# mLSTM cell and gelu layer on one core: DRAM copies moved from the up to the end of the down projection, and a new order of the down's steps

## The chip, the core and the metric

The kernel runs on one core of a Trainium2 chip. A core has a matrix engine (TensorE, in the profile PE, with PEld for its weight loads), a vector engine (VectorE, DVE), an activation engine (ScalarE, ACT), a general engine (GpSimd, POOL) and SyncE (SP), which here issues every DMA. Each engine runs its own instructions strictly in the order in which the program lists them, and waits on semaphores for the others. SP is such a queue too: a DMA that has to wait keeps back every DMA listed behind it.

The metric is the device time of one execution in microseconds (us). The kernel before took 484.46 us, the median of 3 runs (484.13 to 487.07).

## The reference

An mLSTM cell for 4 batches, 8 heads, 768 time steps and a head dimension of 40, and behind it a layer that widens 320 to 2048, applies the exact gelu and comes back to 320:

```python
for t in range(S):
    m_new = np.maximum(f_gate[:, :, t] + m, i_gate[:, :, t])
    f_stab = np.exp(f_gate[:, :, t] + m - m_new)
    i_stab = np.exp(i_gate[:, :, t] - m_new)
    C = f_stab[..., None, None] * C + i_stab[..., None, None] * einsum('bhd,bhe->bhde', vt, kt)
    n = f_stab[..., None] * n + i_stab[..., None] * kt
    y[:, :, t] = sigmoid(o_gate[:, :, t]) * (C @ qt) / maximum(abs(n . qt), 1.0)
x = y.transpose(0, 2, 1, 3).reshape(3072, 320)
out = gelu_exact(x @ w_in) @ w_out
```

## The kernel before

**Chunks.** Time is cut into 6 chunks of 128 steps. For each chunk the cell is computed in matrix form for each of the 4 batches: scores of keys and queries, times a weight matrix with a mask; times the values; plus what the carried state gives. Its output (512 rows of x) then goes through the layer: the up projection (`up`, L818: TensorE at L839 and L850, gelu on ScalarE at L854) and the down projection (`down_steps`, L907: TensorE at L920). While the down of chunk c runs, the cell of chunk c+1 is worked in between its products. For c = 1 to 4 the order of that mixture is written out by hand in the string DOWN (L37); the last down has no cell beside it. The profile shows the five pairs one after another: up and down of chunk 1 from 129.4 to 200.3 us, of chunk 2 to 274.5, of chunk 3 to 350.0, of chunk 4 to 419.5, and of chunk 5 to the end. What stands before 129.4 (the order FRONT) is the same before and after.

**The letters of DOWN.** Each word is a step, with a batch number behind it where it has one:

- F: the next of 14 products of the down (16 groups of rows summed in a Strassen-like scheme, 8 matmuls by 2 tiles). Every second F ends a bank of PSUM, and what empties it follows: F2 a copy on ScalarE (`p1`), F4 an addition on VectorE (`p6`), F6 a copy (`p2`), F8, F10, F12, F14 additions (`p5`, `p7`, `p3`, `p4`). `p3` and `p4` also issue two output DMAs each on SP (`send`, L887).
- M: the mask (GpSimd, L421). W: the exponentials of the weights (ScalarE, L447). G: the sigmoid of the output gate (ScalarE, L453).
- K and Q: VectorE transposes a batch's keys or queries (L469) from the tile `blocks`, one buffer for the batches 0, 1 and 2. Q of the batches 0 and 1 also issues the loads of the next batch's blocks (4 DMAs, L170); Q0 to Q2 and D3 weigh the values (GpSimd, L504). L3 clears a tile for the last batch (GpSimd, L459) and loads its blocks (4 DMAs). B3 loads the last batch's weights (L187). K and Q of the batches 0 and 1 do not stand in DOWN: they run in the up before it (`turns`), K0 and Q0 in its middle, K1 and Q1 later.
- S (scores of two batches: L533 on TensorE, then 8 multiplications on VectorE, L539), C (the old state times the queries, L588), h (the state's update: L599 on TensorE, L608 and L614 on VectorE, L612 on GpSimd). V: the values (TensorE L635, one addition on VectorE L643). V0 also issues the loads of the last batch's keys and values (4 DMAs, L152), into the buffers that batch 0 had.
- Y: the division (ScalarE L650, GpSimd L651 and L652, VectorE L656 and L657, then a copy on ScalarE, L664). X: the transposes of the result (TensorE L675, then a copy on ScalarE, L685). R: two operations of VectorE that split it in two parts (L698, L699). Z: two instructions of a sum of weights (VectorE, L753), in the down of chunk 1 alone. N: two subtractions on VectorE (`sum_late`, L950) that F11 and F12 need.
- j (`load_next`, L481): the loads of the first batch's blocks of the chunk after, 4 DMAs.

**The copies.** The blocks are read from a copy of k and q in DRAM with a fitting layout. `copy_chunk(c)` (L157) makes it for one chunk with 16 DMAs on SP (L162), 80 KB each. Chunk 2 is copied around the first up. In the up of chunk c the copy for chunk c+2 is issued (L864), for c = 1, 2 and 3: behind K0 and Q0 and behind the loads that the last down put off (`later_loads`: weights L190, keys and values L152 and L154, output gates L154), and ahead of the blocks that Q1 and L3 load.

Of the kernel before, what the change touches and what calls it, by code (L numbers as in the profile page):

```python
# [34 lines left out]
    K K B8 F J K F F J K F F F R0 X1 J J K F J F K X2 F J  # L35
    K F J Y3 K F R1 e J F Z B9 B10 F X3 R2 Z R3 F p"""
DOWN = """  # L37
    Z F M1 M0 W0 W1 F L3 Z Z S0 C0 F h0 B3 K2 G1 V0 Q2 M2 W2 G2 F K3 F M3 G0 V1 F W3 Q3 S2 D3 Y0 C2 h2 F Z G3 N F
    Y1 X0 F V2 F V3 X1 Y2 R0 F Y3 R1 j F X2 R2 F X3 R3 F"""


@with_exitstack
def kernel(
# [20 lines left out]
    NCH = S // L  # L64
# [92 lines left out]
    def copy_chunk(c, batches=range(B)):  # L157

        for b in batches:
            for i, src in enumerate((k, q)):  # L160
                for hip in range(2):
                    nc.sync.dma_start(out=kq_d[c - 2][b, hip].rearrange("(m i x t) d -> i x m (t d)", m=NP, i=2, x=16)[i],  # L162
                                      in_=src[b, hip::2, c * L:(c + 1) * L, :].rearrange("m (x t) d -> x m (t d)", x=16))

    def load_blocks(n, to):

        c, b = divmod(n, B)
        for hip in range(2):
            for d, w in ((0, 32), (32, D - 32)):
                nc.sync.dma_start(out=to[64 * hip + d:64 * hip + d + 32].rearrange("t m i (g w) -> t (m i g) w", w=32)[:, :, 0:w],  # L170
                                  in_=kq_d[c - 2][b, hip, :, d:d + w].rearrange("(x t) d -> t x d", t=32))
# [235 lines left out]
    class Cell:  # L407
# [73 lines left out]
        def load_next(self):  # L481
            if self.c + 1 < NCH:
                load_blocks((self.c + 1) * B, by_block)

        def weigh_last(self, b):
            if self.c < NCH - 1:
                self.weigh_values(b)
# [235 lines left out]
    def split_weight():  # L723
        i = len(w_lo)
        if i in (0, 3, 5, 8):
            two = shared([P, NX, 2, WP // 2], F32R, "w_in_hi")
            w_hi.extend([two[:, 0], two[:, 1]])
        elif i == 2:
            two = shared([P, 2, 2, WP // 2], F32R, "w_rest_hi")
            w_hi.append(two[:, 0])  # L730
            rest_two.append(two[:, 1])
        elif i == 7:
            w_hi.append(rest_two[0])
        w = w_all[i]
        nc.scalar.activation(out=w_hi[i], in_=w, func=AF.Copy, scale=PART * 2.0 ** -12)
        w_lo.append(w_f(F32R, "w_in_lo"))
        nc.vector.scalar_tensor_tensor(out=w_lo[i], in0=w_hi[i], scalar=-BASE * 2.0 ** 12, in1=w, op0=OP.mult, op1=OP.add)
# [3 lines left out]
    def join_weight(i):  # L741
        w_mid[i] = raw.tile([P, 2, WP // 2], F32R, name="w_in_mid", tag="pow") if i % 5 in (1, 4) else w_f(F32R, "w_mid")
        nc.vector.tensor_tensor(out=w_mid[i], in0=w_hi[i], in1=w_lo[i], op=OP.add)  # L743
# [22 lines left out]
    def hidden_sums(g, f0, f1):  # L766

        (a11, a21), (_, a22) = [[g.t[:, HF * e + f0:HF * e + f1, HT * h:HT * (h + 1)] for h in range(2)]
                                for e in range(2)]
        s1, s2 = [t[f0 // (HF // 2)][:, f0 % (HF // 2):f0 % (HF // 2) + f1 - f0, :] for t in (g.s1, g.s2)]  # L770
        nc.vector.tensor_tensor(out=s1, in0=a21, in1=a22, op=OP.add)  # L771
        nc.vector.tensor_tensor(out=s2, in0=s1, in1=a11, op=OP.subtract)
        nc.vector.tensor_tensor(out=a21, in0=a11, in1=a21, op=OP.subtract)
# [44 lines left out]
    def up(g, sums_too, turns):  # L818

        def split_to(i):  # L820
            while len(w_lo) <= i:
                split_weight()

        def pair(f, ahead):

            at = [f // 2 * 5 + f % 2 * 3 + x for x in range(NX)]
            split_to(at[1])
            for i in at:
                if i not in w_mid:
                    join_weight(i)  # L830
            pus = [[pool.tile([P, TG], F32, name="pu", tag=tag) for e in range(2)]
                   for pool, tag in (((ps_h, "h"), (ps_mm, "a")), ((ps_tr, "tr"), (ps_mm, "b")))[f % 2]]
            ahead()
            mid = [w_mid.pop(i) for i in at]
            for n, (w, x) in enumerate((([w_hi[i] for i in at], parts["x"]), ([w_lo[i] for i in at], parts["x_lo"]), (mid, parts["x_all"]))):
                for i in range(2):
                    for e in range(2):
                        for k in range(NX):
                            nc.tensor.matmul(pus[i][e], w[k][:, e, i * P:(i + 1) * P], x[:, k, :],  # L839
                                             start=(n == 0 and k == 0), stop=False, skip_group_check=True)  # L840
            return pus

        def rest(u, banks, order):
            mid = w_mid.pop(5 * u + 2)
            for i in order:
                pu = banks[i]
                for n, (w, x) in enumerate(((w_hi[5 * u + 2], parts["x"]), (w_lo[5 * u + 2], parts["x_lo"]), (mid, parts["x_all"]))):
                    for e in range(2):
                        r = halves[e]
                        nc.tensor.matmul(pu[e], w[r, i // 2, i % 2 * P:(i % 2 + 1) * P], x[r, NX, :], start=False,  # L850
                                         stop=(n == 2), skip_group_check=True)

        def out(i, e, pu):
            nc.scalar.activation(out=g.t[:, HF * e + i, :], in_=pu[e], func=AF.Gelu, scale=4097.0)  # L854

        if c == 1:
            copy_chunk(2, range(1, B))
        b0 = pair(0, lambda: split_to(4))
        b1 = pair(1, lambda: join_weight(2))
        for step in turns[:1]:  # L860
            step()
        while later_loads:
            later_loads.pop(0)()
        if c + 2 < NCH:  # L864
            copy_chunk(c + 2)
        rest(0, b0 + b1, (0, 1, 2, 3))
        split_to(6)
        join_weight(5)
        join_weight(6)
        for i, pu in enumerate(b0 + b1):  # L870
            for e in range(2):
                out(i, e, pu)
        for step in sums_too[:5]:
            step()
        b2 = pair(2, lambda: split_to(9))
        hidden_sums(g, 0, 2)
        b3 = pair(3, lambda: (hidden_sums(g, 2, 4), join_weight(7)))
        for step in turns[1:] + sums_too[5:]:
            step()
        rest(1, b2 + b3, (2, 3, 0, 1))  # L880
        for i, e in ((2, 0), (2, 1), (3, 0), (0, 0), (1, 0), (3, 1), (0, 1), (1, 1)):
            out(4 + i, e, (b2 + b3)[i])
        hidden_sums(g, HF - 2, HF)
        hidden_sums(g, HF - 4, HF - 2)
# [125 lines left out]
    for c in range(1, NCH):  # L1010
        g, later, steps = Hidden(True), [], {}
        if c + 1 < NCH:
            steps = cell_steps(c + 1, "MWGTscVYXRLKQDCBSjh", g)
        up(g, weight_sum(1) + weight_sum(2) + weight_sum(3) if c == 1 else [], [lambda b=b: (steps["K"](b), steps["Q"](b)) for b in range(2)] if steps else [])
        if c == 1:
            later = weight_sum(4)
        products, late = down_steps(c, g)
        steps |= dict(F=in_turn(products), Z=in_turn(later), N=late)
        play("F " * 14 if c + 1 == NCH else DOWN, steps)
# [30 lines left out]
```

## Time and profile before

| | |
|---|---|
| median of 3 runs | 484.46 us |
| the profiled execution's own time | 483.82 us |
| its span, first to last instruction | 482.0 us |
| mean granted TensorE clock | 0.996 |
| TensorE busy | 469.9 us (97%) |
| VectorE busy | 316.1 us (66%) |
| ScalarE busy | 244.1 us (51%) |
| GpSimd busy | 78.8 us (16%) |
| an up (chunk 2, 3, 4) | 28.72 us each |

The profile is of one execution. Its own time is 1.8 us above its span, which is what lies around the first and last instruction. "Idle, released by" tells who ended a wait. The chain of waits follows the run back from its last instruction; "SPq" in it is SP issuing DMAs. PE busy does not mean that TensorE is at its peak, only that a matmul was under way.

### The profile page before, as it was taken

What the parts mean: (1) busy time and instruction counts of PE and PEld (TensorE: products, weight loads), DVE (VectorE), ACT (ScalarE), POOL (GpSimd) and SP (SyncE); (2) the same over time, 40 slices, a digit from 0 to 9 for tenths busy, and PEclk for the clock granted to TensorE, in tenths of its full rate; (3) what the DMA queues carried; (4) which work ended last, traced back from release to release, by engine and by line L of the source; (5) the groups of instructions that cost most, each with busy time, mean ns of one, the idle gap of its engine ahead of it and who ended that gap; (6) DMA issues with size and microseconds to landing.
All of it is one profiled execution on the core that took longest, in us unless ns stands there. A gap on an engine that the chain in (4) does not pass through costs nothing.

```text
span 482.0 us, 12967 instructions
## 1 busy us (share of the span) xinstructions
PE 469.9 (97%) x5380; PEld 406.7 (84%) x5380; DVE 316.1 (66%) x694; ACT 244.1 (51%) x521; POOL 78.8 (16%) x120
## 2 busy tenths in 40 slices
PE   8899999999999999999989999989999999999997
PEld 8787888777777999977979977979977899977997
DVE  7899699797869958644747735647545767624321
ACT  6977999844532973231962211954303784211300
POOL 3002020000030223102324202215101412100000
PEclk9999999999999999999999999998999999999999
DMA  9997972278854640169590139582029930100001
GB/s 176 201 222 171 237 177 69 84 194 182 187 113 117 99 59 3 55 103 201 119 136 6 56 72 202 126 135 30 29 49 214 116 74 3 47 12 0 1 1 54
DMA packets 172475, 49.79 MB, mean 103 GB/s; under 512 B 154400, under 2 KB 165952, under 8 KB 172416
## 3 DMA queue, kind: packets, MB, share of 16 engines
q1 hardware_dynamic: 172416, 48.97, 50.7%
q8 instruction: 42, 0.69, 0.6%
q14 instruction: 17, 0.14, 0.1%
HBM read 44.82 MB, written 9.37 MB: 112 GB/s over the span
## 4 chain that ended last, share of the span: by engine, by line
PE 84%; SPq 6%; DVE 4%; DMA 2%; issue 2%; ACT 1%; POOL 0%; DVEq 0%
PE po L920 29%; PE pu L839 21%; PE po L897 7%; PE pu L784 6%; PE pu L850 5%; PE ph L635 3%; PE ps L533 2%; SPq L162 2%; PE px L675 2%; PE pu L790 2%; DMA blocks<-kq_d 2%; PE ps L517 2%; SPq L170 1%; PE pf L588 1%; SPq L154 1%
## 5 line engine op out<-in xcount | busy, mean ns | idle before, releaser
L854 ACT ACTIVATE g<-pu 128x512 f32<-128x512 f32 x80 | 40.8, 616 | 107.7 <-PE pu L850 107.6
L920 PE MATMUL po<-w_out,g 128*128 128x160 f32 x640 | 92.7, 301 | 0.0
L920 PEld LDWEIGHTS po<-w_out,g 128*128 128x128 f32 x640 | 87.9, 190 | 2.3 <-ACT g L854 1.8
L920 PE MATMUL po<-w_sums,sums 128*128 128x160 f32 x320 | 47.0, 303 | 0.0
L920 PEld LDWEIGHTS po<-w_sums,sums 128*128 128x128 f32 x320 | 43.9, 190 | 0.6
L839 PE MATMUL pu<-x_hi,w_in_hi 128*128 128x512 f32 x160 | 41.4, 401 | 0.0
L839 PE MATMUL pu<-x_lo,w_in_lo 128*128 128x512 f32 x160 | 40.6, 396 | 0.0
L447 ACT ACTIVATE W<-W,aT 128x128 f32<-128x128 f32 x128 | 38.7, 388 | 0.4
L839 PEld LDWEIGHTS pu<-x_hi,w_in_hi 128*128 128x128 f32 x160 | 29.4, 188 | 8.2 <-ACT g L854 1.9
L839 PEld LDWEIGHTS pu<-x_lo,w_in_lo 128*128 128x128 f32 x160 | 30.1, 188 | 7.2
L421 POOL TENSOR_SCALAR_AFFINE_SELECT W<-W 128x1024 f32<-128x1024 f32 (+2 forms) x20 | 22.2, 1111 | 80.6 <-DMA W<-M_d 72.6
L897 PE MATMUL po<-w_out,g 128*128 128x320 f32 x128 | 35.2, 433 | 0.0
L743 DVE TENSOR_TENSOR w_in_mid<-w_in_hi,w_in_lo 128x512 fp32r<-128x512 f32 x20 | 13.8, 688 | 29.5 <-PE pu L839 29.5
L771 DVE TENSOR_TENSOR sums<-g 128x512 f32<-128x512 f32 x20 | 13.7, 687 | 28.8 <-ACT g L854 28.8
L897 PEld LDWEIGHTS po<-w_out,g 128*128 128x128 f32 x128 | 24.0, 190 | 9.6
L839 PE MATMUL pu<-x_all,w_mid 128*128 128x512 f32 x80 | 31.6, 395 | 0.0
L839 PE MATMUL pu<-x_all,w_in_mid 128*128 128x512 f32 x80 | 31.6, 395 | 0.0
L504 POOL TENSOR_TENSOR vw<-vb,ewT 128x328 f32<-128x328 f32 x12 | 9.5, 789 | 133.4 <-DMA vb<-in_v_dram 57.8
L784 PE MATMUL pu<-first_x,w_in 128*128 128x256 f32 x128 | 29.0, 382 | 0.0
L933 DVE TENSOR_TENSOR o_sb<-po,o_sb 128x320 f32<-128x320 f32 (+1 forms) x27 | 12.4, 459 | 25.2 <-PE po L920 21.2
L539 DVE TENSOR_TENSOR W<-ps,W 128x256 f32<-128x256 f32 (+1 forms) x48 | 18.1, 415 | 14.1 <-PE ps L533 10.7
L784 PEld LDWEIGHTS pu<-first_x,w_in 128*128 128x128 f32 x128 | 23.8, 190 | 3.4 <-DVE w_in L387 0.3
(183 smaller groups left out, 877.1 us busy)
## 6 DMA issues: line engine op xcount, KB each, us to landing
W<-M_d SPq DMA_DIRECT2D x16, 512.0 KB, 5.3
bits<-in_moe_w_in_dram SPq DMA_DIRECT2D x20, 256.0 KB, 4.2
bits<-in_moe_w_out_dram SPq DMA_DIRECT2D x16, 320.0 KB, 3.3
blocks<-kq_d SPq DMA_DIRECT2D x32, 128.0 KB, 3.0
ob<-in_o_gate_dram SPq DMA_DIRECT2D x24, 160.0 KB, 4.1
out_dram<-o_sb SPq DMA_DIRECT2D x24, 160.0 KB, 1.9
kq_d<-in_k_dram SPq DMA_DIRECT2D x32, 80.0 KB, 2.4
kq_d<-in_q_dram SPq DMA_DIRECT2D x32, 80.0 KB, 2.5
```

Of the source, the lines that this page charges most:

```text
L421: nc.gpsimd.affine_select(out=x, in_=x, compare_op=OP.is_ge, fill=1.0e30, base=base, pattern=[[0, H], [1, x.shape[2]]], channel_multiplier=-1)
L447: nc.scalar.activation(out=W[n][:, h, :], in_=src, func=AF.Exp, scale=-1.0, bias=aT[:, self.c, r:r + 1])
L539: nc.vector.tensor_tensor(out=w[r, :, t], in0=ps[i][hip][r, :, t], in1=w[r, :, t], op=OP.mult)
L635: nc.tensor.matmul(ph[r, h, :], Pm[:, h, r], vb[turn_of(n)][:, h, :], start=True, stop=True)
L743: nc.vector.tensor_tensor(out=w_mid[i], in0=w_hi[i], in1=w_lo[i], op=OP.add)
L771: nc.vector.tensor_tensor(out=s1, in0=a21, in1=a22, op=OP.add)
L784: nc.tensor.matmul(banks[-1][e][:, i - i0, :], in_tile(i, x)[:, e, i % 2 * P:(i % 2 + 1) * P], first_x[:, x, t0:t1], start=(x == 0 and i = ...
L839: nc.tensor.matmul(pus[i][e], w[k][:, e, i * P:(i + 1) * P], x[:, k, :], start=(n == 0 and k == 0), stop=False, skip_group_check=True)
L850: nc.tensor.matmul(pu[e], w[r, i // 2, i % 2 * P:(i % 2 + 1) * P], x[r, NX, :], start=False, stop=(n == 2), skip_group_check=True)
L854: nc.scalar.activation(out=g.t[:, HF * e + i, :], in_=pu[e], func=AF.Gelu, scale=4097.0)
L897: nc.tensor.matmul(po[b], g.t[:, f, b * L:(b + 1) * L], w_out[:, f, :], start=(f == 0), stop=(f == NF - 1))
L920: nc.tensor.matmul(bank[at][:, i, :], lhs(j, t), rhs(j), start=(first and i == 0 and j == 0), stop=(i == n - 1 and j == HF - 1), skip_grou ...
```

## The change

Two things change. The order DOWN is new, and the copies for the chunks 4 and 5 are issued in `load_next` behind the first blocks, so at the end of the downs of chunk 1 and 2. The copy for chunk 3 stays in the up of chunk 1. In the up of chunk 2 and 3 no copies are left.

```diff
 DOWN = """
-    Z F M1 M0 W0 W1 F L3 Z Z S0 C0 F h0 B3 K2 G1 V0 Q2 M2 W2 G2 F K3 F M3 G0 V1 F W3 Q3 S2 D3 Y0 C2 h2 F Z G3 N F
-    Y1 X0 F V2 F V3 X1 Y2 R0 F Y3 R1 j F X2 R2 F X3 R3 F"""
+    F Z M0 Z W0 F M1 L3 W1 S0 C0 M2 F B3 K2 F G1 h0 Q2 D3 G2 V0 K3 Z W2 F Q3 V1 M3 G0 Z F G3 W3 S2 C2 h2 F Y0 F V2
+    F Y1 X0 N Y2 F R0 V3 F X1 F Y3 j X2 R1 F R2 X3 R3 F"""
...
         def load_next(self):
             if self.c + 1 < NCH:
                 load_blocks((self.c + 1) * B, by_block)
+            if self.c + 2 < NCH:
+                copy_chunk(self.c + 2)
...
-        if c + 2 < NCH:
-            copy_chunk(c + 2)
+        if c == 1:
+            copy_chunk(3)
         rest(0, b0 + b1, (0, 1, 2, 3))
```

With the F's numbered, TensorE's order in a down goes from F1 F2 S0 C0 F3 h0 V0 F4 F5 V1 F6 S2 C2 h2 F7 F8 X0 F9 V2 F10 V3 X1 F11 F12 X2 F13 X3 F14 to F1 F2 S0 C0 F3 F4 h0 V0 F5 V1 F6 S2 C2 h2 F7 F8 V2 F9 X0 F10 V3 F11 X1 F12 X2 F13 X3 F14. In the old order j stands ahead of F12 and its two sends, in the new one behind them. D3 now stands ahead of V0: it weighs what the values' buffer holds at that moment, which is batch 0's values and not yet the last batch's.

## The prediction

> **What bounds the kernel now.** I read the chain of waits first, then cut the span into its ups and downs, then read SP's own queue in time order. The page's shares of the chain:
>
> ```profile
> PE 84%; SPq 6%; DVE 4%; DMA 2%; issue 2%; ACT 1%; POOL 0%; DVEq 0%
> ```
>
> TensorE sets the end, with one foreign part: 6% of the chain is SP issuing. Where does that cost TensorE time? The table of stretches, the downs of chunk 1 to 4 (length, then busy time by engine, the granted clock, the DMA engines' share):
>
> ```profile
> 158.10:200.28 42.18, 42.18 (x815) 40.73 (x813) 33.08 (x79) 26.70 (x62) 12.70 (x20) 1.00 0.31 51
> 229.00:274.45 45.45, 43.44 (x815) 41.28 (x813) 30.25 (x68) 26.68 (x62) 14.53 (x20) 1.00 0.42 77
> 303.17:350.00 46.83, 44.46 (x814) 42.53 (x813) 29.64 (x68) 26.68 (x62) 13.82 (x19) 0.96 0.40 75
> 378.72:419.48 40.76, 40.76 (x751) 39.32 (x749) 27.79 (x60) 26.69 (x62) 10.07 (x13) 1.00 0.26 46
> ```
>
> The first and the last are full of matmuls from end to end. The last is shorter because its cell makes no state update: 64 matmuls fewer. The second and third hold the same 815 matmuls as the first and take 3.27 and 4.65 us longer. That, 7.92 us, is all that TensorE loses in the four downs. The chain in the second, in order of time (start, us, what):
>
> ```profile
> 226.46 0.83 SPq L162
> ...
> 243.93 3.17 DMA blocks<-kq_d
> ...
> 248.31 0.63 DVE qT L469
> ...
> 248.98 1.40 PE ps L533 x42
> ```
>
> Read it upwards: the scores S2 wait for the transposes of the last batch's blocks, these for a DMA, and that was issued late because SP had just issued the 16 copies. SP's queue beside it, in chunk 2, in chunk 4 (which has no copies), and in the down of chunk 1:
>
> ```profile
> 172.26 2.39 SPq L170 DMA_DIRECT2D blocks<-kq_d  x4
> ...
> 197.47 4.44 SPq L887 DMA_DIRECT2D out_dram<-o_sb  x4
> 208.71 2.68 SPq L170 DMA_DIRECT2D blocks<-kq_d  x4
> ...
> 238.02 6.46 SPq L170 DMA_DIRECT2D blocks<-kq_d  x8
> ...
> 271.64 0.84 SPq L887 DMA_DIRECT2D out_dram<-o_sb  x2
> ...
> 371.74 4.60 SPq L154 DMA_DIRECT2D ob<-in_o_gate_dram  x3
> 376.82 6.43 SPq L170 DMA_DIRECT2D blocks<-kq_d  x8
> ```
>
> In chunk 4 the eight loads follow the gates at 376.82, 1.9 us before the down begins, and nothing is lost. In chunk 2 they begin at 238.02, 9.0 us after it has begun. The copies took 226.46 to 238.02, 11.6 us.
>
> **The part that moves the copies.** It takes the 11.6 us from in front of the loads of Q1 and L3 in the ups of chunk 2 and 3, and brings them to the end of the downs of chunk 1 and 2. I follow each queue they pass. Below, r is the time since a down's first F (158.1 in chunk 1), u the time since an up began (200.28 in chunk 2).
>
> On SP, j now stands behind F12's two sends. F12 ends at about r = 37.4 (worked out below), the addition that the sends wait for at 38.1, they take 0.84, j's four loads 2.4 as at 172.26: until 41.4. The copies follow, 11.6, to 53, then F14's two sends, 0.84. The down is over at 42.5 to 43, so SP is free in the next up at u = 11. There the loads that Q0 issues began at 208.71, u = 8.4: they come 2.6 us later, and I let the whole series behind them come 2.6 us later. Q1's loads then begin at 226.46 + 2.6 = 229.1 instead of 238.02, L3's at 231.7, and with the chain's 3.2 us from the last issue they land by about 235 and 237.5, r = 6 and 8.5. They are due at r = 10 and 15 (below). GpSimd's and ScalarE's queues hold no DMA.
>
> j's loads themselves were issued at r = 14.2 (172.26) and now at 39: they land by r = 45, u = 2. They are due when K0 runs:
>
> ```profile
> 207.38 0.71 DVE L469 STREAM_TRANSPOSE kT<-blocks 128x512 f32<-128x512 f32 x1
> ```
>
> That is u = 7.1, so 5 us are left, also in the ups of chunk 3 and 4. F14's sends go out 11 us later, into output tiles next written a whole up later. Cost on the path: none. Gain: the two losses. The third down's loss is not all waiting, though:
>
> ```profile
> 321.64 0.43 PE L533 MATMUL ps<-qT,kT 64*64 64x128 f32 x2
> ...
> 324.26 0.44 PE L533 MATMUL ps<-qT,kT 64*64 64x128 f32 x2 [2.19 <-DVE far L643]
> 324.88 2.61 PE L533 MATMUL ps<-qT,kT 64*64 64x128 f32 x56 [0.17 <-DVE qT L469]
> ```
>
> The same stretch in the table of stretches:
>
> ```profile
> 324.00:330.00 6.00, 5.56 (x162) 5.21 (x163) 2.96 (x8) 3.84 (x10) 2.82 (x5) 0.72 0.66 87
> ```
>
> From 321.64 to 324.88 is waiting, 3.1 us beside the four matmuls done; the other 1.5 of 4.65 is the granted clock, 0.72 in those six us. I take it that the low clock follows from the gap and goes with it, since the second down, with gaps under 1 us, kept 1.00. "TensorE: Matmul & The Clock Gate" of the Trainium skill, The HAM clock gate, says that the clock falls after at least one idle window of about 3.4 us; the gap here is 2.2 us, so by that rule the dip would have another cause and could stay, and the sum would be 1.5 us higher. The trace shows the dip right behind the shorter gap, and I go by the trace.
>
> **The part that reorders.** What matters is whether an engine falls behind TensorE. TensorE's pieces, from the chain of chunk 1:
>
> ```profile
> 158.18 4.54 PE po L920 x32
> ...
> 176.66 1.50 PE ps L533 x64
> 178.15 0.92 PE pf L588 x64
> 179.07 0.74 PE pf L599 x32
> ...
> 187.60 2.37 PE po L920 x16
> ...
> 195.87 2.17 PE po L920 x16
> ```
>
> A pair of F's takes 4.54, one alone 2.37, behind the small X transposes 2.17; V takes about what h does, 0.74, X 0.3. The new order has eleven runs of F's where the old has ten; summed piece by piece that is 0.05 us more per down, 0 to 0.2 by the rows (4.74 for two alone against 4.54): 0.2 in all. The new places follow: h0 at r = 11.5, S2 at 18.5, h2 at 20.9, F11 at 32.5, F12's end 37.4, X3 at 39.9, the end 42.4.
>
> F2's copy on ScalarE, then VectorE's durations, with the row that gives its delay behind TensorE (200.59 against 200.28, 0.3):
>
> ```profile
> 166.29 0.40 ACT L937 COPY o_sb<-po 128x320 f32<-128x320 f32 x1
> ```
>
> ```profile
> 163.20 1.49 DVE L753 TENSOR_TENSOR t<-w_out,w_sums 128x160 f32<-128x160 f32 x6
> 164.62 3.27 DVE L539 TENSOR_TENSOR W<-ps,W 128x256 f32<-128x256 f32 x8
> ...
> 168.00 0.63 DVE L608 TENSOR_TENSOR far<-pf,gT 128x164 f32<-128x164 f32 x2
> 168.55 0.65 DVE L614 TENSOR_TENSOR state<-state,pf 40x164 f32<-40x164 f32 x2
> ...
> 170.37 0.71 DVE L469 STREAM_TRANSPOSE kT<-blocks 128x512 f32<-128x512 f32 x1
> 171.11 0.50 DVE L643 TENSOR_TENSOR far<-ph,far 128x328 f32<-128x328 f32 x1
> ...
> 180.72 1.74 DVE L539 TENSOR_TENSOR g<-ps,g 128x256 f32<-128x256 f32 x4 [1.03 <-issue]
> ...
> 192.95 0.49 DVE L657 TENSOR_TENSOR ob<-ob,den 128x320 f32<-128x320 f32 x1 [0.57 <-POOL ob L652]
> 193.36 0.55 DVE L698 SCALAR_TENSOR_TENSOR x_lo<-px,x_hi 128x384 fp32r<-128x384 f32 x1
> ...
> 200.59 0.49 DVE L933 TENSOR_TENSOR o_sb<-po,o_sb 128x320 f32<-128x320 f32 x1 [0.63 <-PE po L920]
> ...
> 258.21 2.36 DVE L950 TENSOR_TENSOR g<-g,sums 128x1024 f32<-128x1024 f32 x2
> ```
>
> Four deadlines:
>
> - *S2, due at 18.5.* F2's copy now stands between W0 and W1 on ScalarE, 0.4 us; S0's multiplications end at 9.8 + 0.4 = 10.2, then K2. F4's addition now stands ahead of h0's work and holds it to 11.8 (F4's end, 11.5, and 0.3). Behind it in one run: 0.4, h0's eight operations 2.3, Q2 0.6, V0's 0.4, K3 and Q3 1.25, V1's 0.4: 17.2, in chunk 1 with one Z 17.7. Slack 1.3 and 0.8 us. No cost, but it is the tightest of the early ones.
> - *h2's keys, due at 21.3.* V0's loads wait for h0 and V0 on TensorE (13.0) and now, for the values, for D3 on GpSimd, which itself no longer waits for them. The keys' two DMAs come first and are issued by 14.4 at the copies' 0.7 each; the row below, of the keys' tile, gives at most 5.9 to landing: 20.3.
>
> ```profile
> DMA to landing us min/median/max: 3.5/5.3/5.9
> ```
>
> - *F11, due at 32.5, needs N.* S2's last multiplications start at 22.6 in chunk 1 (180.72); G3 ahead of W3 on ScalarE makes it 23.0, so they end at 24.75. h2's work, Y0, F8's, V2's and Y1's operations follow (2.3, 0.8, 0.4, 0.4, and Y1's wait for GpSimd), to about 30.0; N takes 2.36, to 32.4. F11 reads the second half of what N writes only in its fifth matmul. No cost, up to 0.5 if it waits for both halves.
> - *X3, due at 39.9, needs the bank that R1 empties.* F12's addition begins at 37.7, Y3 ends at 38.9, R1's two operations at 39.85, and a signal has to pass: X3 comes 0.1 to 0.2 late. In the old order R1 stood ahead of F12. I take 0.12 per down, 0.5 us in all; bounds 0, and 0.6 a down (a Y3 that misses GpSimd by the 0.57 of the row at 192.95), 2.4.
>
> Sum, against the profiled execution's own time: 483.82 - 7.92 + 0.2 + 0.5 = 476.6 us. The median of the runs shown is 0.64 above that execution, so a median after may stand at 477.2; that is inside the range.
>
> **Rivals.** (1) *The order eats part of it.* The last three deadlines miss by more than worked out: F11 0.5 and X3 0.6 in each of four downs, 4.4 us instead of 0.5, makes 480.5; half of it 478.5. For it: slacks of 0 to 1 us put together from rows of another order. Against: VectorE is busy for only 30 of 45 us in a down. (2) *The slow clock stays*: 476.6 + 1.5 = 478.1, if the 0.72 has a cause other than the gap. Against: it stands directly behind the only gap above 1 us in these downs. (The rule of the Trainium skill named above speaks for this one.) (3) *The change doesn't do what it says.* The loads of Q1 and L3 stay late for another reason: the DMA engines, not SP, are the limit, and the series takes in the copies' time all the same. Then the losses stay: 483.8 + 0.7 = 484.5. Against: chunk 4, with the same series and no copies, is on time by 1.9 us. (4) *Slower.* The copies now stand ahead of what the next down needs first: Q0's blocks, three of its four weight tiles, its keys and values. If copies and series slow each other so that the series is not 2.6 but d us late, the blocks of Q1 are late from d = 7 on; VectorE's run behind K2 takes up 2 us more, then passes the delay to S2, one for one, in the downs of chunk 2 and 3. From d = 9 on it costs 2 us for each; at d = 12.6 the gain is gone, 483.8, and d = 16 gives 490.6. For it: the copies are on the same 16 engines. Against: in the old ups the same copies ran beside gates and blocks at 0.7 us an issue.
>
> **How the numbers follow.** Forecast 0.70, with a range of its own of 475.4 (no cost of the order, the sum of the split at 0, and 0.5 for a difference of runs) to 478.0; rival 1 0.13; rival 2 0.04; rival 3 0.07; rival 4 0.06. The range of 8 in 10 takes the forecast, rival 2 and most of rival 1: 475.4 to 479.6. A difference of 1%, 4.8 us, is about what a measurement of this kernel can tell from none: faster by more (under 479.6) holds the forecast, rival 2 and most of rival 1, 0.85; within it the rest of rival 1 and most of rival 3, 0.09; slower 0.06.
>
> **What would show it.** In the profile after: the downs of chunk 2 and 3 as long as that of chunk 1, about 42.4; SP out of the chain there; L170 x8 ahead of or at the start of the down; SP's L162 in the first 11 us of the up; the granted clock at 1.00 behind S2. The reorder is wrong where TensorE idles ahead of S2, L599 of h2, F11 or X3, above all in chunk 1 and 4, which had nothing to gain. The forecast falls if L170 for Q1 begins later than r = 5.

## The result and the profile after

The changed kernel takes 476.36 us, the median of 4 runs (476.2 to 477.38), the kernel before beside it 484.29 us. The ratio is 0.9836, with a 95% interval of 0.9806 to 0.9867: faster by 1.3 to 1.9%. The forecast was 476.6.

The kernel before varies more than its first three runs showed. In the 26 runs beside the experiments it took mostly 480.3 to 485.7 us (medians 482.73 and 483.05 of 13 each), while the changed kernel stayed within 476.2 to 477.4. Two of the 26 stand apart, at 487.9 and 488.2 us with the lowest mean clock (0.986), and are left out of the ratios. Of the others, the nine with a mean granted clock of 0.999 or 1.000 took 480.3 to 482.8 us, the six with 0.993 or less 483.8 to 485.7: the low clock that the prediction read from one profile is in some runs and not in others. Against the two medians the gain is 6.4 to 6.7 us. The ratios below are against the kernel before on the same chip.

The shares of the chain of waits in the changed kernel; SP's 6% has become 1%:

```profile
PE 93%; DVE 3%; SPq 1%; DMA 1%; issue 0%; ACT 0%; DVEq 0%
```

The four downs in the table of stretches of the changed kernel (columns as before: length, busy time by engine, granted clock, share of the DMA engines):

```profile
157.75:199.97 42.22, 42.22 (x815) 40.76 (x813) 32.74 (x79) 25.24 (x61) 14.24 (x20) 1.00 0.28 49
228.68:271.50 42.82, 42.44 (x815) 40.86 (x813) 30.39 (x68) 25.22 (x61) 13.88 (x20) 1.00 0.35 58
300.21:342.43 42.22, 42.22 (x815) 40.75 (x813) 30.30 (x68) 25.23 (x61) 13.45 (x19) 1.00 0.38 63
371.13:411.85 40.72, 40.72 (x750) 39.35 (x749) 27.67 (x60) 25.21 (x61) 9.99 (x13) 1.00 0.24 44
```

Against the stretches of before, the second is 2.63 us shorter (45.45 to 42.82), the third 4.61 (46.83 to 42.22), the first and last are the same to 0.04. The profiled executions differ by 7.62 us (483.82 to 476.20): 7.24 from these two, and 0.36 because the first down begins that much earlier (157.75 against 158.11), behind code that has not changed. The clock in the third is back at 1.00.

SP's queue in the changed kernel, around the seam between the down of chunk 1 and the up of chunk 2, which begins at 199.97:

```profile
195.82 0.83 SPq L889 DMA_DIRECT2D out_dram<-o_sb  x2
196.71 2.65 SPq L170 DMA_DIRECT2D blocks<-kq_d  x4
199.40 1.23 SPq L162 DMA_DIRECT2D kq_d<-in_k_dram  x2
...
208.94 1.23 SPq L162 DMA_DIRECT2D kq_d<-in_q_dram  x2
210.27 1.00 SPq L889 DMA_DIRECT2D out_dram<-o_sb  x2
211.38 2.81 SPq L170 DMA_DIRECT2D blocks<-kq_d  x4
...
224.22 4.52 SPq L154 DMA_DIRECT2D ob<-in_o_gate_dram  x3
228.83 7.40 SPq L170 DMA_DIRECT2D blocks<-kq_d  x8
```

The copies run from 199.40 to 210.2, behind F12's sends and j's loads; then F14's sends; Q0's blocks at u = 11.4; and the eight loads of Q1 and L3 at 228.83, 0.15 us after the down has begun (it had been 9.0).

What is left of a loss is in the second down. TensorE's own list there shows S2 on time and then a wait inside h2, behind the 21st of its 32 matmuls:

```profile
247.15 1.57 PE L535 MATMUL ps<-qT,kT 64*64 64x128 f32 x64
248.54 1.09 PE L590 MATMUL pf<-state,qT 64*64 64x41 f32 x64
249.56 0.61 PE L601 MATMUL pf<-vw,kb 128*40 128x41 f32 x21
250.56 0.43 PE L601 MATMUL pf<-vw,kb 128*40 128x41 f32 x11 [0.38 <-issue]
```

"Issue" means that it waited for nothing that the profile shows. The chain of the kernel before goes on at this place, behind the rows that the prediction shows, like this:

```profile
251.55 0.74 POOL vw L504
...
252.33 0.31 PE pf L599 x5
252.64 0.91 issue
253.55 0.43 PE pf L599 x10
```

So the 3.27 us lost in that down were not all a wait for the last batch's blocks. h2 began 1.5 us late there (22.4 us into the down, against 20.9 in the down of chunk 1). The other 1.8 us arose inside h2, where TensorE waited 0.44 us for D3 (vw, on GpSimd) and 0.91 us for "issue". In the changed kernel h2 begins on time, at 20.9, and loses 0.6. What the "issue" wait is, the last experiment shows.

### The profile page after: what moved, and what is told of

Same layout as the page of the kernel before. It is cut to its first block, busy times and chain, and to the rows that moved or that the text cites. A ratio compares the mean times of both kernels' runs of the same rounds, so it can differ in the third digit from the quotient of the medians.

```text
span 474.4 us, 12960 instructions
## 1 busy us (share of the span) xinstructions
PE 465.1 (98%) x5380; PEld 403.4 (85%) x5380; DVE 315.4 (66%) x694; ACT 238.2 (50%) x517; POOL 78.2 (16%) x120
## 4 chain that ended last, share of the span: by engine, by line
PE 93%; DVE 3%; SPq 1%; DMA 1%; issue 0%; ACT 0%; DVEq 0%
PE po L922 33%; PE pu L841 24%; PE po L899 7%; PE pu L852 6%; PE pu L786 6%; PE ph L637 4%; PE ps L535 3%; PE pu L792 2%; PE px L677 2%; PE pf L590 2%; SPq L154 1%; PE ps L519 1%; PE pf L601 1%; PE pf L557 1%; PE pt L497 1%; DMA bits<-in_moe_w_in_dram 1%
## 5 line engine op out<-in xcount | busy, mean ns | idle before, releaser
L922 PE MATMUL po<-w_out,g 128*128 128x160 f32 x640 | 94.2, 302 | 0.0
L922 PE MATMUL po<-w_sums,sums 128*128 128x160 f32 x320 | 45.9, 302 | 0.0
L421 POOL TENSOR_SCALAR_AFFINE_SELECT W<-W 128x1024 f32<-128x1024 f32 (+2 forms) x20 | 23.3, 1175 | 80.3 <-DMA W<-M_d 79.7
L935 DVE TENSOR_TENSOR o_sb<-po,o_sb 128x320 f32<-128x320 f32 (+1 forms) x27 | 12.6, 466 | 34.2 <-PE po L922 30.2
L666 ACT COPY y_rest<-ob 128x128 f32<-128x128 f32 x16 | 4.8, 298 | 54.1 <-DVE ob L659 31.0
```

Of the source, the lines that this page charges most:

```text
L421: nc.gpsimd.affine_select(out=x, in_=x, compare_op=OP.is_ge, fill=1.0e30, base=base, pattern=[[0, H], [1, x.shape[2]]], channel_multiplier=-1)
L922: nc.tensor.matmul(bank[at][:, i, :], lhs(j, t), rhs(j), start=(first and i == 0 and j == 0), stop=(i == n - 1 and j == HF - 1), skip_grou ...
```

## The experiments

**The copies moved, the order left.** The changed kernel with the old string DOWN, in which j stands ahead of F12.

```diff
-    F Z M0 Z W0 F M1 L3 W1 S0 C0 M2 F B3 K2 F G1 h0 Q2 D3 G2 V0 K3 Z W2 F Q3 V1 M3 G0 Z F G3 W3 S2 C2 h2 F Y0 F V2
-    F Y1 X0 N Y2 F R0 V3 F X1 F Y3 j X2 R1 F R2 X3 R3 F"""
+    Z F M1 M0 W0 W1 F L3 Z Z S0 C0 F h0 B3 K2 G1 V0 Q2 M2 W2 G2 F K3 F M3 G0 V1 F W3 Q3 S2 D3 Y0 C2 h2 F Z G3 N F
+    Y1 X0 F V2 F V3 X1 Y2 R0 F Y3 R1 j F X2 R2 F X3 R3 F"""
```

> The copies issued behind the next first blocks, as in the change, but the down's steps in the old order, where j stands ahead of F12. Theory (what was gained is SP's queue: the copies no longer stand ahead of the blocks of Q1 and L3; the order is worth nothing): both losses go, 483.8 - 7.9 = 475.9 us, 475.5 to 476.5; downs of chunk 2 and 3 at 42.2, and SP does the copies from about r = 17 to 28 of the downs, while nothing else is due. Rival (the new order is what gains, or what the move needs): 481 to 484.

476.38 us (476.29 to 476.46), ratio 0.9863 (0.982 to 0.9907). Its profile has SP issue the copies in the middle of the down of chunk 2, with nothing due:

```profile
245.04 1.59 SPq L162 DMA_DIRECT2D kq_d<-in_k_dram  x2
...
255.99 1.23 SPq L162 DMA_DIRECT2D kq_d<-in_q_dram  x2
268.94 4.44 SPq L889 DMA_DIRECT2D out_dram<-o_sb  x4
```

The theory holds. Moving the copies alone gives the whole gain; the new order adds nothing that these runs can tell. The downs of chunk 2 and 3, expected at 42.2 us, take 43.2 and 42.2: the first has an "issue" wait of 0.83 us in h2.

**The order changed, the copies left.** The kernel before with the new string DOWN.

```diff
-    Z F M1 M0 W0 W1 F L3 Z Z S0 C0 F h0 B3 K2 G1 V0 Q2 M2 W2 G2 F K3 F M3 G0 V1 F W3 Q3 S2 D3 Y0 C2 h2 F Z G3 N F
-    Y1 X0 F V2 F V3 X1 Y2 R0 F Y3 R1 j F X2 R2 F X3 R3 F"""
+    F Z M0 Z W0 F M1 L3 W1 S0 C0 M2 F B3 K2 F G1 h0 Q2 D3 G2 V0 K3 Z W2 F Q3 V1 M3 G0 Z F G3 W3 S2 C2 h2 F Y0 F V2
+    F Y1 X0 N Y2 F R0 V3 F X1 F Y3 j X2 R1 F R2 X3 R3 F"""
```

> The new order of the down's steps, the copies in the up as before. Theory (SP's queue): the blocks of Q1 and L3 land as late as before, at about r = 15 and 18 to 20, and in the new order more stands behind K2 on VectorE, so S2 waits 2.6 to 3.2 us and the rest of the losses stays: 482 to 484.5. Rival (the order gains): 476 to 478. The granted clock behind S2: under 0.9 in a down whose gap is above 2 us, 1.00 where it is under 1 us.

482.86 us (482.03 to 484.18), ratio 1.0003 (0.9978 to 1.0029): no change. From its table of stretches, the downs of chunk 2 and 3 and the six us from 324 on, in S2 of the latter and behind it; from TensorE's list, the gaps ahead of that S2:

```profile
230.14:274.86 44.72, 42.93 (x815) 41.04 (x813) 30.26 (x68) 25.22 (x61) 13.84 (x20) 1.00 0.39 73
303.57:350.30 46.73, 44.23 (x814) 42.43 (x813) 30.34 (x68) 25.22 (x61) 12.52 (x19) 0.96 0.38 74
...
324.00:330.00 6.00, 4.96 (x160) 4.84 (x161) 2.79 (x8) 3.84 (x10) 2.67 (x4) 0.72 0.16 26
```

```profile
323.44 0.43 PE L533 MATMUL ps<-qT,kT 64*64 64x128 f32 x2 [1.33 <-DVE far L643]
325.04 2.01 PE L533 MATMUL ps<-qT,kT 64*64 64x128 f32 x56 [1.17 <-DVE far L643]
```

Without the move both losses stay. S2 goes on 1.7 and 3.0 us late in the two downs, where 2.6 to 3.2 were expected. The clock falls again, behind gaps of 1.33 and 1.17 us close together; I had expected that only behind a gap above 2 us. In the down of chunk 2, with one gap of 1.17, it stays at 1.00.

**SP's time or the transfers?** The kernel before, with the copies of chunk 4 and 5 cut in two: the same bytes at the same place, twice the DMAs.

```diff
-                    nc.sync.dma_start(out=kq_d[c - 2][b, hip].rearrange("(m i x t) d -> i x m (t d)", m=NP, i=2, x=16)[i],
-                                      in_=src[b, hip::2, c * L:(c + 1) * L, :].rearrange("m (x t) d -> x m (t d)", x=16))
+                    to = kq_d[c - 2][b, hip].rearrange("(m i x t) d -> i x m (t d)", m=NP, i=2, x=16)[i]
+                    by = src[b, hip::2, c * L:(c + 1) * L, :].rearrange("m (x t) d -> x m (t d)", x=16)
+                    for m in (slice(0, NP // 2), slice(NP // 2, NP)) if c > 3 else (slice(0, NP),):
+                        nc.sync.dma_start(out=to[:, m], in_=by[:, m])
```

> The kernel before, with the copies for chunk 4 and 5 cut into 32 DMAs of 40 KB instead of 16 of 80 KB, at the same place and with the same bytes. Theory (what delays the blocks is the time that SP needs to issue, 0.6 to 0.7 us each): the blocks come 11.6 us later, S2 waits that much longer in the downs of chunk 2 and 3, 484 + 23 = 507 us, more where the clock falls in the longer gaps. Rival (the transfers on the DMA engines delay them): the same bytes, the same time, 484 to 486.

503.97 us (2 runs), ratio 1.0435 (1.0352 to 1.0518): 21 us longer where 23 were expected. SP's queue in chunk 2, first and last copies and the loads behind them, and who TensorE waited for in the run (us in total, times, longest):

```profile
225.87 2.73 SPq L165 DMA_DIRECT2D kq_d<-in_k_dram  x4
...
245.87 2.50 SPq L165 DMA_DIRECT2D kq_d<-in_q_dram  x4
248.47 6.06 SPq L172 DMA_DIRECT2D blocks<-kq_d  x8
```

```profile
PE ps L535 <- DVE qT L471: 17.9, 2, 9.3
```

A DMA of 40 KB takes SP as long as one of 80 KB, 0.6 us, so the loads come 10.5 us later (248.47 against 238.02). It is SP's time that delays them here, not the bytes.

**How much slack has the new place?** The same cut in the changed kernel (the diff is the one above).

> The changed kernel, with the copies for chunk 4 and 5 cut into 32 DMAs of 40 KB. SP reaches Q0's blocks at about u = 22.6 instead of 11, so the series in the ups of chunk 2 and 3 is 14.2 us later than before the change instead of 2.6. Theory (the slack of the new place ends at a delay of about 9 us, then one for one): S2 waits about 5 us in each of two downs, 476.4 + 10.4 = 487, 483 to 491. Rival (at the end of the down the copies cost nothing, however long): 476 to 477.

490.26 us (2 runs), ratio 1.0151 (1.0078 to 1.0223): slower than before the change. SP's queue in the up of chunk 2, then VectorE and TensorE in the down, which begins at 228.56:

```profile
221.62 2.72 SPq L172 DMA_DIRECT2D blocks<-kq_d  x4
...
241.16 7.20 SPq L172 DMA_DIRECT2D blocks<-kq_d  x8
```

```profile
247.29 0.71 DVE L471 STREAM_TRANSPOSE kT<-blocks 128x512 f32<-128x512 f32 x1 [3.30 <-DMA blocks<-kq_d]
```

```profile
252.02 0.68 PE L537 MATMUL ps<-qT,kT 64*64 64x128 f32 x2 [4.92 <-DVE far L647]
253.61 2.62 PE L537 MATMUL ps<-qT,kT 64*64 64x128 f32 x56 [0.91 <-DVE far L647]
```

Counted from the start of the down, the eight loads are issued 12.45 us later than in the changed kernel (12.6 against 0.15), and S2 is 6.55 us late (253.61, due at 228.56 + 18.5). So the changed kernel has 12.45 - 6.55 = 5.9 us of slack left there. In the down of chunk 3 the loads are 10.3 us later and S2 5.1 late, so 5.2 are left. This is rival 4 of the prediction made real, along the path named there: K2 first, then VectorE's run behind it.

**D3 behind V0.** The changed kernel, with D3 where it weighs the last batch's own values.

```diff
-    ... h0 Q2 D3 G2 V0 ... G3 W3 S2 C2 h2 ...
+    ... h0 Q2 G2 V0 ... G3 W3 S2 D3 C2 h2 ...
```

> The changed kernel with D3 back behind S2, so that it weighs the last batch's values and not what the buffer held before. Theory: the values' two DMAs are issued from about r = 13.6 to 15.8 and land 4 to 6 us later, r = 18 to 21.5; D3 takes 0.74 and h2's second half is due at 21.3, so h2 waits 0 to 1 us in the downs of chunk 1 to 3: 476.4 to 479. Rival (that D3 no longer waits for a transfer carries part of the gain): above 479. Rival (nothing hangs on it): 476.0 to 476.8.

476.29 us (476.11 to 476.96), ratio 0.9871 (0.983 to 0.9912). D3 in the down of chunk 1, on GpSimd:

```profile
175.62 0.89 POOL L506 TENSOR_TENSOR vw<-vb,ewT 128x328 f32<-128x328 f32 x1 [3.06 <-DMA vb<-in_v_dram]
```

It waits 3.06 us for the values and is still done over 2 us before h2 needs it; the wait of up to 1 us that the theory had expected in h2 does not come. No part of the gain hangs on D3's place. With D3 here, the state update uses the last batch's own values, which the changed kernel leaves out in the downs of chunk 1 to 3 (it weighs batch 0's). The right place costs nothing, so this one, or the old order with the copies moved, is the kernel to keep.

**j ahead of F12.** The changed kernel with its copies in the middle of the down, as in the old order.

```diff
-    ... R0 V3 F X1 F Y3 j X2 ...
+    ... R0 V3 F j X1 F Y3 X2 ...
```

> The changed kernel with j ahead of X1 and F12, where SP does not wait for F12's addition: the copies are issued from about r = 17 to 28 as in the old order, and Q0's blocks in the next up at their old time, 2.4 us earlier than in the change. Theory (2.4 us of delay were covered by slack): the same time, 475.9 to 476.8. Rival (the copies at the seam of down and up cost something): under 475.5.

477.09 us (476.12 to 478.0), ratio 0.9888 (0.9837 to 0.9939). The median lies above the 475.9 to 476.8 expected; two of the four runs, 477.61 and 478.0, have a mean clock of 0.996, the other two are within it. Beside the changed kernel on the same chip (the next run but one, 0.987, 0.983 to 0.991) the two cannot be told apart. No cost of the seam shows.

**The copies behind Q1's loads.** The kernel before, with the copies of chunk 4 and 5 later in the same ups.

```diff
-        if c + 2 < NCH:
-            copy_chunk(c + 2)
+        if c == 1:
+            copy_chunk(3)
...
         for step in turns[1:] + sums_too[5:]:
             step()
+        if 1 < c and c + 2 < NCH:
+            copy_chunk(c + 2)
```

> The kernel before with the copies for chunk 4 and 5 issued in the same ups but behind Q1's loads, so that only L3's loads (the last batch's blocks), the last batch's weights, keys and values stand behind them. Theory (the chain ran over the last batch's blocks): K2 is on time, K3 as late as before, about r = 17.5, so most of the losses stays: 481 to 484. Rival (it is batch 2's blocks that bind): 476 to 478.5.

482.89 us (480.84 to 485.45), ratio 1.0002 (0.9974 to 1.0029). The transposes K2 and K3 on VectorE in the down of chunk 2:

```profile
241.06 0.71 DVE L469 STREAM_TRANSPOSE kT<-blocks 128x512 f32<-128x512 f32 x1
...
247.44 0.71 DVE L469 STREAM_TRANSPOSE kT<-blocks 128x512 f32<-128x512 f32 x1 [4.14 <-DMA blocks<-kq_d]
```

K2 no longer waits, K3 does, and nothing is gained. In the old order it was the last batch's blocks, L3's loads, that bound.

**The changed kernel again**, on the chip of the last three.

> The changed kernel once more, to stand beside the variants on the same chip: 475.9 to 477.0.

476.38 us (476.19 to 476.54), ratio 0.987 (0.983 to 0.991).

**The wait inside h2.** The changed kernel with more warming matmuls at the start.

```diff
     nc.vector.memset(w_out[:, 0, 0:P], 0.5)
-    warm(6)
+    warm(16)
```

> The changed kernel with ten more matmuls among those that warm TensorE at the very start, where it waits for data anyway. It is about the 0.4 to 1.0 us in the down of chunk 2 in which TensorE waits, behind the 21st of h2's 32 matmuls, for nothing that the profile shows. Theory (it is tied to the count of TensorE's instructions, as if the next ones had not arrived): the wait moves ten matmuls forward, to behind the 11th. Rival (it is tied to data, such as the last batch's keys): it stays behind the 21st. Either way 476 to 477.5 us.

476.56 us (one run). The ten matmuls are twenty in the profile (the first group has 32 where it had 12). TensorE's list in the down of chunk 2 now has no wait:

```profile
249.47 1.09 PE L590 MATMUL pf<-state,qT 64*64 64x41 f32 x64
250.50 0.81 PE L601 MATMUL pf<-vw,kb 128*40 128x41 f32 x32
```

Neither side had this: the wait neither stayed nor showed up further ahead. Counting TensorE's instructions in the traces tells what it is. These instructions come by DMA too: every trace has 42 transfers of 16 KB of the kind "instruction" on queue q8. In all eight profiles with the wait, exactly 5,825 of TensorE's recorded instructions (matmuls and weight loads above all) stand ahead of it, and it ends 1.3 to 1.5 us after the 22nd of these transfers has landed. A second such wait, of 0.2 to 0.8 us at about 93 us, has 2,241 instructions ahead of it in ten profiles, and ends 1.2 to 1.4 us after the eighth transfer has landed. Between the two lie 14 transfers and 3,584 instructions, 14 times 256. So TensorE waits there for the next block of 256 of its own instructions.

With twenty matmuls and their weight loads more ahead, the edge of the same block falls at the start of h2, 2.5 us after its transfer has landed, and there is nothing to wait for. The theory had the cause right; that the wait would only move was wrong.

## Why the prediction was right

- **The place and the cause of the loss**: right in the main. It was SP's time ahead of the blocks. The copies alone, moved, give the gain; the order alone gives none; twice the DMAs with the same bytes make it 21 us worse. Of the 3.27 us in the second down, though, only 1.5 had been lost when h2 began; the rest arose inside h2, in part as the wait for TensorE's own instructions. The chain that I read had these rows, just behind the last that I took.
- **SP's queue after the change**: Q0's blocks were expected at u = 11 and came at 11.4, Q1's loads at 229.1 and came at 228.83.
- **The gain of 7.92 us** was 7.24 in the profiled execution. The loss of the second down did not go to zero: 0.6 us stayed, most of it the "issue" wait in h2, which I had counted as part of the wait for the blocks. Most runs of the kernel before are shorter than the profiled one; since the move takes the loss away whatever its size, the time after could be forecast better than the gain.
- **The cost of the order, 0.2 + 0.5**: the 0.5 was not paid. The 0.2 was 0.05 a down. Against the old order with the copies moved, the downs of chunk 1 and 3 are 0.06 us longer (42.22 against 42.16), that of chunk 4 is not. VectorE and TensorE in the down of chunk 1 of the changed kernel, at three of the deadlines (V1's addition for S2, N for F11, R1 for X3):

```profile
175.01 0.46 DVE L645 TENSOR_TENSOR far<-ph,far 128x328 f32<-128x328 f32 x1
...
187.53 2.35 DVE L952 TENSOR_TENSOR g<-g,sums 128x1024 f32<-128x1024 f32 x2
...
196.85 0.55 DVE L701 TENSOR_TENSOR x_all<-px,x_hi 128x384 fp32r<-128x384 f32 x1
```

```profile
197.57 0.38 PE L677 MATMUL px<-ident,ob 128*128 128x128 f32 x2
```

V1's addition ends at r = 17.7, as worked out. N ends at 189.9, r = 32.1 (32.4 expected). R1 ends at 197.4, and X3 starts 0.2 later without a wait; I had R1 end at r = 39.85, and it was 39.65. So 476.6 is closer to 476.2 than its terms were: a gain 0.7 too large, costs up to 0.7 too large, and 0.36 from the start of the kernel, on which nothing was forecast. That the first two cancel is luck.
- **The clock**: the dip went with the gap, and it was there again in the order-alone kernel, behind its gaps (0.72). The 1.5 us of rival 2 did not stay.
- **Rival 4's point**: the series was d = 2.7 us late in the changed kernel (228.83 against 226.46 less the 0.36 of the earlier start), and 5.9 were left, so it decides at d = 8.6; 9 was forecast.

## What to carry to other kernels

A queue that issues DMAs is a resource like an engine: find the time at which what stands in it is next due, and put long runs of issues that nobody waits for behind that and not ahead. Cutting a transfer into more DMAs can cost the queue in proportion to their number: here one of 40 KB took it as long as one of 80. A loss read from one profile is that of one run; look at how the runs scatter before you promise it as a gain. Before a change bundled with a reordering is credited, run the two alone: here one of them did everything.

## What the hardware showed

- The granted clock fell to 0.72 over six us behind two idle gaps of 1.33 and 1.17 us. Seen closer, it is 0.50 for 3.41 us and then 1.00 again, in that kernel and in the one before. The Trainium skill, "TensorE: Matmul & The Clock Gate", The HAM clock gate, gives at least one idle window of about 3.4 us for that. The dip is as long as that window, but no single gap there is. In the 3.41 us ahead of the dip TensorE was busy for 1.22 us in the kernel before and for 1.14 in this one, so the window need not be wholly idle.
- The kernel before, which waits for a DMA in two downs, scattered over more than 5 us from run to run (480.3 to 485.7); the eight runs of the changed kernel lie within 1.2 us. That the waits are the reason was not tested.
- The wait inside h2 stood behind the same matmul in eight profiles: 0.3 to 0.4 us in the changed kernel, both times, and in the one with D3 behind V0, and 0.6 to 1.0 us in the five others. It was not there in the two kernels with 32 copies, nor with twenty matmuls more ahead of it. It is a wait for a block of 256 of TensorE's own instructions, 16 KB that come by DMA. In the three profiles with the short wait the DMA engines were all but idle from 246 to 250 us (a share of 0.01), in the five others they were busy (0.60 to 1.20); that this makes the block late fits, and was not tested.
